# A scheduler's model of PSUM banks and the shared port, and a new early order, in a retention and feed-forward kernel

## The chip, the cores and the metric

One core of one Trainium2 chip. The metric is the device time of one execution in microseconds; a kernel's time is the median of its runs. TensorE (PE) multiplies matrices into PSUM, VectorE (DVE), ScalarE (ACT) and GpSimd (POOL) work element by element, and SyncE (SP) issues the DMAs.

## What is computed

The reference, cut to what matters (8 batches, 8 heads, 576 positions, head size 64; 4608 tokens of 512, inner width 2048):

```
scores = q @ k.T / sqrt(64)                       # per batch and head
ret    = scores * D        # D[i,j] = gamma_h**(i-j) for i >= j, else 0
x      = (ret @ v), heads side by side            # 4608 x 512
h      = x @ w_in                                 # 4608 x 2048
P      = a0 + a1*h + a2*h**2 + a3*h**3
Q      = 1 + |b0|*|h| + |b1|*h**2
out    = (P / (Q + 1e-6)) @ w_out                 # 4608 x 512
```

## The kernel before

**Tiling.** Tokens are taken in 36 units of 128; four units make a batch `b` of 512 tokens (nine batches). Retention is done unit by unit with a running state `S_sb` that fades from one unit to the next. The feed-forward part runs in steps `(b, f)`: one 512-token batch by one of 16 slices of 128 inner columns. Each step has a first product (`gemm1` and `gemm1_lo`, 12 matmuls of 128x512 into a PSUM bank `h`), a chain of elementwise instructions on ScalarE, VectorE and POOL, and a second product (`gemm2` and `gemm2_lo`, 12 matmuls into the accumulators `acc`). The order of the steps is: batch 0, slices 0 to 7; batch 1, all 16; batch 0, slices 8 to 15; then batches 2 to 8. Operands are split into a high and a low part (`xhi`, `xlo`, `w[0]`, `w[1]`, `g[0]`, `g[1]`), hence three times four matmuls.

**Weights** come as 64-bit words and are made into two parts on the chip: `begin` and `digit` (ScalarE), `join` (VectorE, `c<-bits`), `high_part` (ScalarE, `w<-c`), `low_part` (POOL, `w<-c,w`).

**The elementwise chain of an early step** (`feed_forward`, line 717; early means step number `i` below 24): `p_begin` (ScalarE, `p<-h`), `size` (ScalarE, `u<-h`), `p_mul` and `p_mul2` (VectorE, `p<-p,fac,h`), `v_line`, `v_mul`, `log`, `exp`, `quot`, `check`, `better`, then the high part `g_hi` (`g<-p`) and the low part `g_lo` (`g<-p,g`) of the result. Early steps keep the value of `v_line`, `log`, `exp` and `check` in the `h` bank itself, and so hold the bank until `better` is done. `V_POOL` names the early steps whose `v_mul` runs on POOL (then `v_line` writes to `v` and not to the bank). Steps with `i % 4 >= 2` among the early ones use two more banks of the pool `ps_w`. After step 23 those two banks are given to the late retention visits (unit 8 onwards, `late_visit`, line 640): the first visit has all the last instructions of such steps in its list of what it follows (`held`).

**The early units** 0 to 7 are done in `attention` (line 384): `scores`, `decay`, `outputs`, `cross` (with the state so far), then `keep_hi` (ScalarE, `xhi<-ps`), `keep_lo` and `grow` (VectorE, `xlo<-ps,xhi` and `S_sb<-S_sb,ps`), all on one PSUM tile, and `fade` on POOL.

**What sets the order.** No order is written by hand. Every piece of work is a `Task` with an engine (or a choice of two), a cost, a due time and the tasks that it follows. `Plan.run` (line 127) plays the five engines' queues forward with these costs: for each engine it works out the earliest start of each open task, takes among those within `SLACK` of the earliest the one with the smallest due time, and then the engine whose choice starts first; the task's instructions are emitted there and then, in this order. So a wrong estimate of a start changes the order in which the instructions stand in the queues; it never removes a wait that correctness needs. The due time of an early step's task is the step's number plus a constant of `DUE`; later steps use `STEADY`; the units use `FIRST`; weights `LEAD` and `AHEAD`; loads go in the order of `LOADS` (a number is the q/k half of a unit, a number with v its k/v half, w0 to w11 the first weight slices, gq the factors). `HOLD` says by how much longer a task must wait before the second engine of its choice may take it. `LAG` is what is added to a task's end before another may follow it.

**The port** (lines 58 and 157 to 159). Tasks marked `shared` use the SBUF port that VectorE and POOL have in common. Before, a VectorE task may start `PORT` = 0.33 us after POOL's shared task ends, a POOL task at once when VectorE's ends. **The banks:** before, nothing in the planner says that ScalarE and VectorE may not be on one PSUM bank together; `size` and `p_mul` both follow `p_begin` alone.

All instructions are issued through one helper, so nearly all rows of the profile show line 77; the names of the tiles tell them apart.

Of the kernel before, what the change touches and what calls it, by code (L numbers as in the profile page):

```python
# [33 lines left out]
EARLY = 8  # L34
DENSE = 8
VISITS = ()
V_POOL = (0, 1, 2, 3, 4, 5, 10, 11, 17)
IN_BANK = 24
WARM = 11
AHEAD = -5.306  # L40
REACH = 7.4
FIRST = (-62.53, -91.46, -10.84, -82.81, -41.01, -22.3, -1.16, -35.8)
UNITS = (20.48, 2.58, -2.5)
LATE = {'scale': -1.0, 'decay': 0.201, 'middle': 0.3, 'grow': 0.524, 'fade': 0.6, 'keep_hi': 0.3, 'keep_lo': 0.5}
LEAD = -2.163
CNV = 3
SHIFT = 60
LOADS = 'gq 0 mask 1 0v 2 1v 2v 3 w0 5 3v 5v w2 w1 w5 4 w4 6 w3 w6 4v w9 w7 w11 w10 7v 7 6v w8'.split()


def begin_of(name):
# [3 lines left out]
LAG = {'PE': 0.21, 'ACT': 0.138, 'DVE': 0.118, 'POOL': 0.08, 'SP': 0}  # L55
BACK = {'PE': 0.21, 'ACT': 0.0, 'DVE': 0.0, 'POOL': 0.0, 'SP': 0.0}
ENTER = {'PE': 0.03, 'ACT': 0.0, 'DVE': 0.0, 'POOL': 0.045, 'SP': 0.0}
PORT = 0.33
FETCH = ((4.8, 1.0), (15.5, 1.1))
DUE = {'p_begin': -0.998, 'size': 1.908, 'p_mul': -0.347, 'p_mul2': 5.296, 'v_line': 1.475, 'v_mul': 1.541, 'log': 3.284, 'exp': -0.985, 'quot': 1.963, 'check': 2.017, 'better': -1.338, 'g_hi': 1.445, 'g_lo': -1.676, 'gemm2': 4.596, 'begin': -0.512, 'digit': 1.055, 'join': -0.091, 'high_part': 1.387, 'low_part': 6.778, 'scale_q': 0.308, 'scale_v': 1.347, 'scores': 2.952, 'decay': 0.786, 'outputs': 6.305, 'cross': -5.06, 'keep_hi': -5.352, 'keep_lo': 3.008, 'grow': -0.794, 'fade': 1.051}  # L60
STEADY = {'p_begin': 0.5, 'size': 0.727, 'p_mul': 0.7, 'p_mul2': 0.93, 'v_line': 0.797, 'v_mul': 0.806, 'log': 1.578, 'exp': 1.838, 'quot': 1.6, 'check': 1.65, 'better': 0.79, 'g_hi': 1.888, 'g_lo': 2.167, 'gemm2': 3.44}
HOLD = {('POOL', 'scale_v'): 8.559, ('DVE', 'p_begin'): 0.394, ('DVE', 'high_part'): 0.99, ('DVE', 'g_hi'): 3.232, ('DVE', 'keep_hi'): 1.752, ('DVE', 'g_lo'): 106.303, ('DVE', 'low_part'): 1.696, ('POOL', 'v_mul'): 3.234, ('DVE', 'scale_q'): 1.067}
SLACK = {'PE': 0.19, 'ACT': 0.283, 'DVE': 0.2, 'POOL': 0.006, 'SP': 0.301}

ADJ = {}
# [3 lines left out]
class InOrder:  # L69


    def __init__(self, tc, engine):
        self.tc, self.engine = tc, engine
# [24 lines left out]
class Task:  # L98


    def __init__(self, due, ways, after, takes, gives):
        self.due, self.ways, self.takes, self.gives = due, ways, list(takes), list(gives)
        self.after = [t for t in after if t is not None]
        self.next, self.open, self.end, self.engine = [], 0, None, None


class Plan:
# [4 lines left out]
        self.tasks = []  # L112
        self.clock = dict.fromkeys(SLACK, 0.0)

    def add(self, engine, due, cost, emit, after=(), takes=(), gives=(), shared=False, other=()):
# [4 lines left out]
        t = Task(due + ADJ.get(len(self.tasks), 0), ways, after, takes, gives)  # L120
        self.tasks.append(t)
        for ring, key in gives:
            n, _ = self.rings[ring].left.get(key, (0, 0.0))
            self.rings[ring].left[key] = n + 1, 0.0
        return t

    def run(self):
        wait = {e: [] for e in SLACK}

        def opened(t):  # L130
            for e in t.ways:
                wait[e].append(t)

        for t in self.tasks:
            t.open = len(t.after)
            for a in t.after:
                a.next.append(t)
            if not t.open:
                opened(t)
        clock = self.clock  # L140
        port = {"DVE": 0.0, "POOL": 0.0}
        dma, landed, left, now, reach = 0.0, [0.75] * OUTSTANDING, len(self.tasks), -2.0, REACH
        while left:
            best = None
            for e, queue in wait.items():
                found = []
                for t in queue:
                    if e != "SP" and t.due > now + reach:
                        continue
                    names = [r for r, _ in t.takes]  # L150
                    ready = [self.rings[r].ready(names[:j].count(r)) for j, r in enumerate(names)]
                    if None in ready:
                        continue
                    _, _, shared, hold = t.ways[e]
                    s = max([0.0, *ready, *(a.end + (-BACK[e] if a.engine == e else ENTER[e]) for a in t.after)]) + hold
                    s = max(s, clock[e], landed[-OUTSTANDING] if e == "SP" else 0.0)
                    if shared:
                        held = port["POOL" if e == "DVE" else "DVE"]
                        s = held + PORT * (e == "DVE") if held > s else s
                    found.append((s, t.due, t))  # L160
                if not found:
                    continue
                until = min(s for s, _, _ in found) + SLACK[e]
                s, _, t = min((f for f in found if f[0] <= until), key=lambda f: f[1])
                if best is None or s < best[0]:
                    best = s, e, t
            if best is None:
                assert reach < 1e6, [(t.due, t.ways) for q in wait.values() for t in q]
                reach *= 2
                continue  # L170
            reach = REACH
            s, e, t = best
            if e == "PE":
                now = max(now, t.due)
            for w in t.ways:
                wait[w].remove(t)
            left -= 1
            cost, emit, shared, _ = t.ways[e]
            t.engine = e
            for ring, _ in t.takes:  # L180
                self.rings[ring].take()
            if e == "SP":
                clock["SP"] = s + 0.47
                fetch = sum(x for at, x in FETCH if dma < at <= max(dma, s + 1.5) + cost)
                dma = max(dma, s + 1.5) + cost + fetch
                t.end = dma + 0.8
                landed.append(t.end)
            else:
                clock[e] = s + cost
                t.end = s + cost + LAG[e]  # L190
                if shared:
                    port[e] = s + cost
            emit()
            for ring, key in t.gives:
                self.rings[ring].give(key, t.end)
            for n in t.next:
                n.open -= 1
                if not n.open:
                    opened(n)
# [3 lines left out]
def retention_ffn(ctx: ExitStack, tc: tile.TileContext, qk, kv, w_in, w_out, masks, factors, out):  # L203
# [25 lines left out]
    add = plan.add  # L229
# [154 lines left out]
    def attention(n, d, gap, got, consts, prev):  # L384
        u, b = n % 9, n // 4
        key = f"u{n}"
# [102 lines left out]
        def at_(x):  # L489
            return d + gap * x  # L490
# [15 lines left out]
        th = add("ACT", at_(DUE["keep_hi"]), 0.495, keep_hi, done, [("xp", b)] if n % 4 == 0 else [], gives,  # L506
                 other=[("DVE", 0.6, keep_hi_v, False)])
# [8 lines left out]
    late_s, bank = {}, {}  # L516
# [200 lines left out]
    def feed_forward(i, b, f, begins, ends):  # L717
        key = b, f
        due = DUE if i < IN_BANK else STEADY
# [149 lines left out]
        tp = add("ACT", i + due["p_begin"], 0.57 if early else 0.66, p_begin, [t1], [("p", key)], other=[("DVE", 0.62, p_begin_v, False)] if early else [])  # L869
        tu = add("ACT", i + due["size"], 0.48, size, [tp], [("u", key)], [] if early else free_h)  # L870
        td = add("DVE", i + due["p_mul"], 0.66 if early else 0.6, p_mul, [tp])
        td = add("DVE", i + due["p_mul2"], 0.66, p_mul2, [td], [], [] if early else free_h)
# [84 lines left out]
    prev = {}  # L957
# [90 lines left out]
```

## Time and profile before

| | |
|---|---|
| median of 3 runs | 903.93 us |
| the three runs | 902.79, 906.62, 903.93 us |
| the profiled execution | 907.24 us, span 905.2 us |
| TensorE's mean granted clock in it | 0.994 of full speed |
| busy: TensorE, VectorE, ScalarE, POOL | 98%, 86%, 70%, 19% of the span |

The profile is one execution. The span runs from its first to its last instruction; the execution's own time holds 2.0 us more around it. Times of rows are microseconds from the start of the span unless marked ns. PE is TensorE's matmuls, PEld its weight loads. "xN" counts instructions; what stands in brackets is the idle time of that engine just ahead and who ended it. A granted clock of 1.00 is 2.4 GHz, 0.50 is 1.2 GHz.

### The profile page before, as it was taken

To read this page: it belongs to the slowest core of one execution; us is meant where nothing else is said; L and a number is where in the kernel's file an instruction comes from. 1 tells how busy PE (TensorE), PEld (TensorE's weight loads), DVE (VectorE), ACT (ScalarE), POOL (GpSimd) and SP (SyncE) were. 2 spreads that over 40 slices of the span, in tenths; PEclk is the share of its full clock that TensorE was granted. 3 is DMA by queue.
4 is the path that set the end of the run, shared out by engine and by line. 5 is a ranking of instruction groups with operands and counts; after the bars stand their busy time and mean duration, and the time that the engine had idled before them with its cause. 6 is when DMAs were issued, how large, how long until landed. Compare 5 with 4: busy or idle time off the path is not lost.

```text
span 905.2 us, 17712 instructions
## 1 busy us (share of the span) xinstructions
PE 887.2 (98%) x7350; PEld 732.3 (81%) x7350; DVE 777.4 (86%) x1175; ACT 636.4 (70%) x1017; POOL 173.0 (19%) x150
## 2 busy tenths in 40 slices
PE   7999999899999999999999999999999999999998
PEld 7777788788878888888888888888888888888886
DVE  4788888878899989998899889888889889888885
ACT  1898998865666667666766677667766777667775
POOL 4766654412201110111100111011100001000000
PEclk9999999989999999999999999999999999999999
DMA  9991000014220112111211131111311021001001
GB/s 355 408 407 61 0 1 1 1 41 159 95 82 20 52 59 94 48 47 59 95 47 48 59 106 48 48 47 48 105 34 38 30 90 47 1 2 46 1 1 47
DMA packets 22208, 67.40 MB, mean 74 GB/s; under 512 B 2160, under 2 KB 4080, under 8 KB 22128
## 3 DMA queue, kind: packets, MB, share of 16 engines
q1 hardware_dynamic: 22128, 66.28, 20.3%
q8 instruction: 57, 0.93, 0.4%
q14 instruction: 23, 0.19, 0.1%
HBM read 56.83 MB, written 9.44 MB: 73 GB/s over the span
## 4 chain that ended last, share of the span: by engine, by line
PE 80%; DVE 9%; ACT 8%; issue 1%; DMA 1%; POOL 1%; SPq 0%; ACTq 0%; DVEq 0%; POOLq 0%
PE h L77 36%; PE acc L77 36%; PE ps L77 8%; DVE p L77 4%; ACT h L77 2%; ACT bits L77 2%; DVE c L77 1%; ACT u L77 1%; DVE v L77 1%; ACT p L77 1%; DVE h L77 1%; DMA qk<-in_qk 1%; ACT w L77 1%; ACT g L77 1%; ACT xhi L77 0%
## 5 line engine op out<-in xcount | busy, mean ns | idle before, releaser
L77 PE MATMUL acc<-w,g 128*128 128x512 f32 x1632 | 396.1, 391 | 1.7 <-ACT o L77 1.4
L77 PEld LDWEIGHTS acc<-w,g 128*128 128x128 f32 x1632 | 307.3, 189 | 67.3 <-ACT o L77 2.2
L77 PE MATMUL h<-xhi,w 128*128 128x512 f32 x1152 | 311.5, 393 | 2.0 <-DVE p L77 1.6
L77 PEld LDWEIGHTS h<-xhi,w 128*128 128x128 f32 x1152 | 213.5, 188 | 48.8 <-DVE p L77 2.8
L77 ACT ACTIVATE p<-h,fac 128x512 f32<-128x512 f32 x141 | 107.6, 763 | 103.7 <-PE h L77 102.7
L77 DVE SCALAR_TENSOR_TENSOR p<-p,fac,h 128x512 f32<-128x512 f32 x192 | 142.2, 744 | 20.4 <-ACT u L77 12.3
L77 PE MATMUL h<-xlo,w 128*128 128x512 f32 x576 | 154.3, 390 | 0.0
L77 PEld LDWEIGHTS h<-xlo,w 128*128 128x128 f32 x576 | 108.1, 188 | 23.1
L77 ACT ACTIVATE g<-p 128x512 fp32r<-128x512 f32 x136 | 85.3, 627 | 54.1 <-DVE p L77 52.0
L77 DVE TENSOR_TENSOR p<-p,h 128x512 f32<-128x512 f32 x120 | 82.2, 685 | 43.2 <-ACT u L77 40.7
L77 ACT ACTIVATE v<-u,absb 128x512 f32<-128x512 f32 x129 | 105.3, 816 | 3.9
L77 ACT ACTIVATE u<-v 128x512 f32<-128x512 f32 x120 | 75.7, 631 | 40.5 <-DVE v L77 40.5
L77 DVE SCALAR_TENSOR_TENSOR p<-p,fac,u 128x512 f32<-128x512 f32 x120 | 92.8, 773 | 9.2 <-ACT u L77 5.4
L77 ACT ACTIVATE u<-h 128x512 f32<-128x512 f32 x144 | 84.9, 590 | 7.9 <-DVE p L77 6.2
L77 DVE TENSOR_TENSOR v<-v,u 128x512 f32<-128x512 f32 x120 | 85.1, 709 | 5.9 <-ACT v L77 5.4
L77 DVE SCALAR_TENSOR_TENSOR v<-v,u 128x512 f32<-128x512 f32 x120 | 90.2, 752 | 0.0
L77 DVE SCALAR_TENSOR_TENSOR p<-v,p 128x512 f32<-128x512 f32 x120 | 84.3, 703 | 3.4
L77 DVE TENSOR_TENSOR g<-p,g 128x512 fp32r<-128x512 f32 x112 | 78.4, 700 | 3.1 <-ACT g L77 1.0
L77 ACT ACTIVATE u<-u 128x512 f32<-128x512 f32 x120 | 75.4, 628 | 2.5
L77 POOL TENSOR_TENSOR qk<-qk,fac 128x512 f32<-128x512 f32 x36 | 49.3, 1369 | 96.8 <-DMA qk<-in_qk 96.5
L77 POOL TENSOR_TENSOR S_sb<-S_sb,fac 128x256 f32<-128x256 f32 x18 | 14.7, 814 | 186.7 <-DVE S_sb L77 186.7
L77 PEld LDWEIGHTS ps<-qk 64*64 64x64 f32 (+1 forms) x1024 | 36.9, 142 | 15.5 <-issue 10.5
(55 smaller groups left out, 743.0 us busy)
## 6 DMA issues: line engine op xcount, KB each, us to landing
qk<-in_qk SPq DMA_DIRECT2D x36, 512.0 KB, 3.9
kv<-in_kv SPq DMA_DIRECT2D x36, 512.0 KB, 5.3
bits<-in_w_in SPq DMA_DIRECT2D x16, 512.0 KB, 10.5
bits<-in_w_out SPq DMA_DIRECT2D x16, 512.0 KB, 10.2
out<-o SPq DMA_DIRECT2D x14, 512.0 KB, 3.0
out<-o SPq DMA_DIRECT2D x8, 256.0 KB, 2.2
x<-in_kv SPq DMA_DIRECT2D x7, 256.0 KB, 4.6
fac<-in_factors SPq DMA_DIRECT2D x1, 301.0 KB, 2.9
```

The costliest lines, as they stand in the source:

```text
L77: return lambda *a, **k: self.tc.keep_in_program_order(method(*a, **k))
```

## The change

The planner gets two new rules and nearly all constants of the early part new values. A task may name a PSUM `bank`; a ScalarE task on a bank may not start before the end of the last VectorE task on it, and the reverse. Named are `keep_hi`, `keep_lo` and `grow` of the early units, and `p_begin`, `size`, `p_mul` and `p_mul2` of every step. `PORT` becomes one constant for each side: a VectorE task may start 0.10 us before the end of POOL's shared task, a POOL task 0.04 us before the end of VectorE's. `V_POOL` goes from nine to seven steps; the order of the loads, the due times of the early steps, of the units and of the weights, and the holds change. `STEADY`, `UNITS`, `LATE`, `SLACK` and the costs stay as they are. No instruction is added; which engine of a pair does a task, and in which place of its queue, is the planner's.

```diff
-V_POOL = (0, 1, 2, 3, 4, 5, 10, 11, 17)
+V_POOL = (1, 2, 3, 9, 11, 17, 22)
-AHEAD = -5.306
+AHEAD = -5.672
-FIRST = (-62.53, -91.46, -10.84, -82.81, -41.01, -22.3, -1.16, -35.8)
+FIRST = (-35.05, -136.62, -18.07, -94.24, -38.78, -4.26, -13.82, -16.04)
-LEAD = -2.163
+LEAD = -3.391
-LOADS = 'gq 0 mask 1 0v 2 1v 2v 3 w0 5 3v 5v w2 w1 w5 4 w4 6 w3 w6 4v w9 w7 w11 w10 7v 7 6v w8'.split()
+LOADS = '0 gq 1 mask 0v 1v 2 w0 2v 3 3v 5v w2 5 w1 w5 4 4v w6 6 w8 w4 w3 6v w7 w11 7v w9 w10 7'.split()
-PORT = 0.33
+PORT = {"DVE": -0.1, "POOL": -0.04}
-DUE = {'p_begin': -0.998, 'size': 1.908, 'p_mul': -0.347, 'p_mul2': 5.296, 'v_line': 1.475, 'v_mul': 1.541, 'log': 3.284, 'exp': -0.985, 'quot': 1.963, 'check': 2.017, 'better': -1.338, 'g_hi': 1.445, 'g_lo': -1.676, 'gemm2': 4.596,
+DUE = {'p_begin': -2.604, 'size': 2.699, 'p_mul': -0.527, 'p_mul2': 6.442, 'v_line': -1.066, 'v_mul': 2.072, 'log': 3.165, 'exp': -2.24, 'quot': 1.803, 'check': 2.07, 'better': -3.106, 'g_hi': 0.509, 'g_lo': -1.637, 'gemm2': 3.917,
...
-HOLD = {('POOL', 'scale_v'): 8.559, ('DVE', 'p_begin'): 0.394, ('DVE', 'high_part'): 0.99, ('DVE', 'g_hi'): 3.232, ('DVE', 'keep_hi'): 1.752, ('DVE', 'g_lo'): 106.303, ('DVE', 'low_part'): 1.696,
+HOLD = {('POOL', 'scale_v'): 8.866, ('DVE', 'p_begin'): 0.153, ('DVE', 'high_part'): 1.173, ('DVE', 'g_hi'): 0.201, ('DVE', 'keep_hi'): 1.352, ('DVE', 'g_lo'): 107.142, ('DVE', 'low_part'): 2.714,
...
+        used = {}
...
+                    if t.bank is not None:
+                        s = max(s, used.get(t.bank, {}).get("ACT" if e == "DVE" else "DVE", 0.0))
                     if shared:
-                        held = port["POOL" if e == "DVE" else "DVE"]
-                        s = held + PORT * (e == "DVE") if held > s else s
+                        s = max(s, port["POOL" if e == "DVE" else "DVE"] + PORT[e])
...
+            if t.bank is not None:
+                used.setdefault(t.bank, {})[e] = t.end
...
-        tl = add("DVE", at_(DUE["keep_lo"]), 0.6, keep_lo, [th], [], gives)
+        tl = add("DVE", at_(DUE["keep_lo"]), 0.6, keep_lo, [th], [], gives, bank=key)
-            tg = add("DVE", at_(DUE["grow"]), 0.33, grow, [to, *done, prev.get("tx")], [], gives)
+            tg = add("DVE", at_(DUE["grow"]), 0.33, grow, [to, *done, prev.get("tx")], [], gives, bank=key)
...
-        td = add("DVE", i + due["p_mul"], 0.66 if early else 0.6, p_mul, [tp])
+        td = add("DVE", i + due["p_mul"], 0.66 if early else 0.6, p_mul, [tp], bank=key)
```

`keep_hi`, `p_begin`, `size` and `p_mul2` get `bank=key` in the same way. In `DUE` and `HOLD` the entries of retention, weights and scaling, left out here, change too.

## Rows read from the trace of the kernel before

**Rows 1.** the page, section 1: busy time and share of the span, by engine
```profile
PE 887.2 (98%) x7350; PEld 732.3 (81%) x7350; DVE 777.4 (86%) x1175; ACT 636.4 (70%) x1017; POOL 173.0 (19%) x150
```

**Rows 2.** waits of TensorE, whole span: us in total, times, longest us
```profile
PE ps L77 <- DVE p L77: 2.7, 1, 2.7
PE ps L77 <- POOL qk L77: 2.4, 2, 1.7
PE ps L77 <- DVE kv L77: 1.8, 1, 1.8
PE ps L77 <- POOL S_sb L77: 1.7, 3, 0.9
PE h L77 <- DVE p L77: 1.6, 2, 0.8
PE acc L77 <- ACT o L77: 1.4, 2, 1.2
```

**Rows 3.** TensorE's timeline: start us, us, instructions [idle before <-releaser]
```profile
104.11 0.73 PE L77 MATMUL acc<-w,g 128*128 128x512 f32 x2 [1.19 <-ACT o L77]
...
177.33 1.15 PE L77 MATMUL ps<-qk 64*64 64x64 f32 x32
181.15 1.12 PE L77 MATMUL ps<-kv 64*64 64x64 f32 x16 [2.67 <-DVE p L77]
182.20 5.49 PE L77 MATMUL acc<-w,g 128*128 128x512 f32 x12
```

**Rows 4.** windows, TensorE: length, busy (instructions), granted clock, DMA share, GB/s
```profile
181.15:182.20 1.05, 1.05 (x17) 0.50 0.00 0
...
184.90:187.60 2.70, 2.70 (x7) 0.50 0.00 0
```

**Rows 5.** the chain that ended last, 195 to 215 us: start us, us, what
```profile
203.54 2.75 PE acc L77 x12
```

**Rows 6.** timeline of all engines, 164 to 192 us, at one bank of `h`
```profile
169.17 0.60 ACT L77 ACTIVATE u<-h 128x512 f32<-128x512 f32 x1 [0.68 <-DVE p L77]
...
169.80 0.75 DVE L77 SCALAR_TENSOR_TENSOR p<-p,fac,h 128x512 f32<-128x512 f32 x1 [0.67 <-ACT u L77]
```

**Rows 7.** waits of all engines, 28 to 180 us
```profile
DVE p L77 <- ACT u L77: 8.4, 12, 1.0
```

**Rows 8.** timeline of all engines, 164 to 192 us, at the shared port
```profile
176.47 1.28 POOL L77 TENSOR_TENSOR w<-c,w 128x512 fp32r<-128x512 f32 x1 [0.92 <-ACT w L77]
176.52 1.78 DVE L77 TENSOR_TENSOR v<-v,u 128x512 f32<-128x512 f32 x1
```

**Rows 9.** groups of VectorE by form, 28 to 180 us: busy us, mean ns
```profile
L77 DVE SCALAR_TENSOR_TENSOR p<-h,p 128x512 f32<-128x512 f32 x23 | 15.9, 692 | 0.8
...
L77 DVE COPY S_sb<-ps 128x256 f32<-128x256 f32 x1 | 0.4, 424 | 0.6 <-PE ps L77 0.6
```

**Rows 10.** timeline of all engines, 0 to 30 us, the first two units
```profile
6.79 1.16 PE L77 MATMUL ps<-qk 64*128 64x128 f32 x16 [0.66 <-POOL qk L77]
...
8.33 1.27 POOL L77 TENSOR_TENSOR qk<-qk,fac 128x512 f32<-128x512 f32 x1 [1.60 <-DMA qk<-in_qk]
...
9.65 1.72 PE L77 MATMUL ps<-qk 64*128 64x128 f32 x16 [1.70 <-POOL qk L77]
```

**Rows 11.** windows, TensorE, behind the first wait; columns as in rows 4
```profile
9.65:12.65 3.00, 3.00 (x30) 0.57 1.03 421
```

**Rows 12.** timeline of all engines, 0 to 30 us, SyncE's issue of the masks
```profile
1.65 0.42 SPq L77 DMA_DIRECT2D mask_sb<-in_masks  x1
```

**Rows 13.** timeline of all engines, 0 to 30 us, VectorE at the fourth unit
```profile
23.28 0.42 DVE L77 TENSOR_TENSOR S_sb<-S_sb,ps 128x256 f32<-128x256 f32 x1 [1.67 <-ACT xhi L77]
23.62 1.71 DVE L77 TENSOR_TENSOR kv<-kv,fac 128x512 f32<-128x512 f32 x2
```

**Rows 14.** windows, all engines: length, busy us of each (instructions)
```profile
40.00:180.00 140.00, 134.83 (x720) 109.46 (x718) 121.42 (x174) 126.09 (x221) 82.85 (x66) 1.00 0.23 92
```

**Rows 15.** VectorE's timeline at the first late visit
```profile
190.43 0.42 DVE L77 COPY S<-ps 128x256 f32<-128x256 f32 x1 [0.83 <-ACT xhi L77]
```

More of the change, by code (lines that the diff above doesn't have):

```diff
@@ L57 @@
 ENTER = {'PE': 0.03, 'ACT': 0.0, 'DVE': 0.0, 'POOL': 0.045, 'SP': 0.0}
-PORT = 0.33
+PORT = {"DVE": -0.1, "POOL": -0.04}
 FETCH = ((4.8, 1.0), (15.5, 1.1))
-DUE = {'p_begin': -0.998, 'size': 1.908, 'p_mul': -0.347, 'p_mul2': 5.296, 'v_line': 1.475, 'v_mul': 1.541, 'log': 3.284, 'exp': -0.985, 'quot': 1.963, 'check': 2.017, 'better': -1.338, 'g_hi': 1.445, 'g_lo': -1.676, 'gemm2': 4.596, 'begin': -0.512, 'digit': 1.055, 'join': -0.091, 'high_part': 1.387, 'low_part': 6.778, 'scale_q': 0.308, 'scale_v': 1.347, 'scores': 2.952, 'decay': 0.786, 'outputs': 6.305, 'cross': -5.06, 'keep_hi': -5.352, 'keep_lo': 3.008, 'grow': -0.794, 'fade': 1.051}
+DUE = {'p_begin': -2.604, 'size': 2.699, 'p_mul': -0.527, 'p_mul2': 6.442, 'v_line': -1.066, 'v_mul': 2.072, 'log': 3.165, 'exp': -2.24, 'quot': 1.803, 'check': 2.07, 'better': -3.106, 'g_hi': 0.509, 'g_lo': -1.637, 'gemm2': 3.917, 'begin': -0.029, 'digit': 0.759, 'join': 0.047, 'high_part': 1.78, 'low_part': 6.704, 'scale_q': 1.543, 'scale_v': 4.227, 'scores': 2.624, 'decay': -1.249, 'outputs': 4.655, 'cross': -2.337, 'keep_hi': -5.517, 'keep_lo': 3.965, 'grow': 0.705, 'fade': 1.485}
 STEADY = {'p_begin': 0.5, 'size': 0.727, 'p_mul': 0.7, 'p_mul2': 0.93, 'v_line': 0.797, 'v_mul': 0.806, 'log': 1.578, 'exp': 1.838, 'quot': 1.6, 'check': 1.65, 'better': 0.79, 'g_hi': 1.888, 'g_lo': 2.167, 'gemm2': 3.44}
-HOLD = {('POOL', 'scale_v'): 8.559, ('DVE', 'p_begin'): 0.394, ('DVE', 'high_part'): 0.99, ('DVE', 'g_hi'): 3.232, ('DVE', 'keep_hi'): 1.752, ('DVE', 'g_lo'): 106.303, ('DVE', 'low_part'): 1.696, ('POOL', 'v_mul'): 3.234, ('DVE', 'scale_q'): 1.067}
+HOLD = {('POOL', 'scale_v'): 8.866, ('DVE', 'p_begin'): 0.153, ('DVE', 'high_part'): 1.173, ('DVE', 'g_hi'): 0.201, ('DVE', 'keep_hi'): 1.352, ('DVE', 'g_lo'): 107.142, ('DVE', 'low_part'): 2.714, ('POOL', 'v_mul'): 2.563, ('DVE', 'scale_q'): 1.924}
 SLACK = {'PE': 0.19, 'ACT': 0.283, 'DVE': 0.2, 'POOL': 0.006, 'SP': 0.301}
@@ L98, with __init__ @@
 class Task:
-    def __init__(self, due, ways, after, takes, gives):
-        self.due, self.ways, self.takes, self.gives = due, ways, list(takes), list(gives)
+    def __init__(self, due, ways, after, takes, gives, bank):
+        self.due, self.ways, self.takes, self.gives, self.bank = due, ways, list(takes), list(gives), bank
         self.after = [t for t in after if t is not None]
@@ L113, in __init__, with add @@
         self.clock = dict.fromkeys(SLACK, 0.0)
-    def add(self, engine, due, cost, emit, after=(), takes=(), gives=(), shared=False, other=()):
+    def add(self, engine, due, cost, emit, after=(), takes=(), gives=(), shared=False, other=(), bank=None):
         ways = {engine: (cost, emit, shared, 0.0)}
@@ L119, in add @@
                 ways[e] = c, f, sh, HOLD[e, emit.__name__]
-        t = Task(due + ADJ.get(len(self.tasks), 0), ways, after, takes, gives)
+        t = Task(due + ADJ.get(len(self.tasks), 0), ways, after, takes, gives, bank)
         self.tasks.append(t)
@@ L506, in attention @@
         th = add("ACT", at_(DUE["keep_hi"]), 0.495, keep_hi, done, [("xp", b)] if n % 4 == 0 else [], gives,
-                 other=[("DVE", 0.6, keep_hi_v, False)])
-        tl = add("DVE", at_(DUE["keep_lo"]), 0.6, keep_lo, [th], [], gives)
+                 other=[("DVE", 0.6, keep_hi_v, False)], bank=key)
+        tl = add("DVE", at_(DUE["keep_lo"]), 0.6, keep_lo, [th], [], gives, bank=key)
         x_ready[b] += [th, tl]
         if u != 8:
-            tg = add("DVE", at_(DUE["grow"]), 0.33, grow, [to, *done, prev.get("tx")], [], gives)
+            tg = add("DVE", at_(DUE["grow"]), 0.33, grow, [to, *done, prev.get("tx")], [], gives, bank=key)
             prev["fade"] = add("POOL", at_(DUE["fade"]), 0.62, fade, [tg], shared=True)
@@ L868, in feed_forward @@
         free_h = [(hring, key)]
-        tp = add("ACT", i + due["p_begin"], 0.57 if early else 0.66, p_begin, [t1], [("p", key)], other=[("DVE", 0.62, p_begin_v, False)] if early else [])
-        tu = add("ACT", i + due["size"], 0.48, size, [tp], [("u", key)], [] if early else free_h)
-        td = add("DVE", i + due["p_mul"], 0.66 if early else 0.6, p_mul, [tp])
-        td = add("DVE", i + due["p_mul2"], 0.66, p_mul2, [td], [], [] if early else free_h)
+        tp = add("ACT", i + due["p_begin"], 0.57 if early else 0.66, p_begin, [t1], [("p", key)], other=[("DVE", 0.62, p_begin_v, False)] if early else [], bank=key)
+        tu = add("ACT", i + due["size"], 0.48, size, [tp], [("u", key)], [] if early else free_h, bank=key)
+        td = add("DVE", i + due["p_mul"], 0.66 if early else 0.6, p_mul, [tp], bank=key)
+        td = add("DVE", i + due["p_mul2"], 0.66, p_mul2, [td], [], [] if early else free_h, bank=key)
         tv = add("ACT", i + due["v_line"], 0.6 if in_bank else 0.71, v_line, [tu, td] if in_bank else [tu], [("v", key)])
```

## The prediction

> **What bounds the kernel now.** I read the page's head first, then what TensorE waited for over the whole span, then the stretch with the longest wait. TensorE is busy for 98% of the span [rows 1], so a new order can win only what TensorE waits for, and what it loses to a lower clock. Its waits after the first load are few [rows 2]: in the first 25 us 2.4 us for POOL's scaling of q and k, 1.8 us for VectorE's scaling of v and 1.7 us for the fading of the state; between 70 and 106 us 1.6 us for an `h` bank that VectorE had not left and 1.4 us for an accumulator that ScalarE had not copied out (most of it at 104 us, [rows 3]); and one wait of 2.7 us. Their sum is 11.6 us; the other rows of the view come to 2.0, and 1.1 of that lies ahead of the first load. So the large second part, from 190 us on, can only be made worse.
>
> The single long wait costs more than its length. At 177.33 us TensorE begins the first late visit (unit 8): its 32 score matmuls end at 178.48, and the next ones need the two `ps_w` banks, which step 23 still holds; it waits 2.67 us for a product `p` on VectorE, step 23's last instruction `better` [rows 3]. From then to 187.60 us the granted clock is 0.50, the lower of the two levels (1.2 GHz), in three stretches in a row, the first and last of them in [rows 4]; the twelve matmuls of one second-product step take 5.49 us there [rows 3], where 2.75 us is the rule [rows 5]. What stood ahead of the fall was an engine that had run 1.15 us in 3.82 us. From 178.48 to 187.61 us are 9.13 us, and the work in it needs 2.75 + 0.55 (the 16 small matmuls at half their 1.12 us) = 3.3 us at full clock. The place costs 5.8 us.
>
> Why was the visit put there? The planner places it where it believes step 23 done. Step 23 is late for two reasons the planner cannot see. **The banks:** `size` of a step on ScalarE waited 0.68 us for the VectorE product on the same `h` bank, and the second VectorE product then 0.67 us for `size` [rows 6]; to the planner `size` and `p_mul` both follow `p_begin` and may run side by side. Between 28 and 180 us VectorE sat idle 8.4 us in 12 places behind a ScalarE write of `u`, which is the `size` that reads the bank [rows 7]. **The port:** `v_mul` of step 24 started on VectorE at 176.52 and took 1.78 us, since POOL held the port from 176.47 to 177.75 [rows 8]; alone an instruction of this size takes 0.69 us [rows 9]. ScalarE, in order, stood behind it, and so did step 23's chain.
>
> **The change part by part.** No wait and no instruction is added: the semaphores between the two engines on a bank are there already [rows 6]. What changes is the planner's arithmetic, and by it the order of every queue.
>
> *Port.* The blocked `v_mul` ends at 178.30; less 0.69 us it began in effect at 177.61, 0.14 us before POOL's end. The old constant lets VectorE begin 0.33 us after it, the new one 0.10 us before: 0.43 us nearer at each blocked instruction. (POOL behind VectorE moves from 0 to 0.04 us before the end: nothing.) The Trainium skill speaks against it: SBUF — State Buffer, section "A bandwidth-pool intuition that's wrong (but worth ruling out)", puts the loser of the port at the holder's end plus about 115 ns. The row has 0.14 us before the end, so the measurement decides. By the page the new constant would be some 0.2 us too early at each blocked instruction; ten such in the early part, an estimate, would be 2 us of VectorE, and the sum would be 1 us higher if half of it reached TensorE.
>
> *The visit at 177 us.* With both effects known the planner should see step 23's end some 2.5 us later and put ahead of the visit what was ready: a whole step of a first or second product, 2.75 us [rows 5], enough to cover 2.67. Bounds: 0 to 5.8 us won; I take 5.0, since the rest of the pattern (new step's ScalarE reads ahead of step 23's logarithm) keeps its due times in the steady table.
>
> *The waits from 70 to 106 us* are of the same kind [rows 2], 3.0 us. Bounds 0 and 3.0; I take half, 1.5, as nothing says which side each falls.
>
> *The first 25 us.* The load list now issues the first q/k before the factors, unit 1's before the masks, and unit 1's v before unit 2's q. The POOL scaling that TensorE waited 1.70 us for is itself waiting for unit 1's load [rows 10]; taking 160 KB of masks from ahead of it gains 0.4 us at the 421 GB/s of the loads there [rows 11]. The masks, issued at 1.65 us [rows 12], then come 1.2 us later (512 KB); I cost that at nothing, since `decay` needs the first scores too, which end at 7.95 [rows 10]; were that cover gone, it would be those 1.2 us at most. The 1.8 us for v is a bank wait once more: the fourth unit's v is scaled at 23.62, behind `grow`, which stands at the head of VectorE's queue for 1.67 us until ScalarE's `keep_hi` has left the same bank [rows 13]. A planner that knows when `grow` can start may scale v in that gap; part of the gap is the wait for the unit's own matmuls, so I take half, 0.9. The half clock behind the first wait (0.57 of full over 3 us of work, [rows 11]) costs up to 1.3 us. Bounds 0 and 6.5 us (1.7 + 1.8 + 1.7 + 1.3); I take 0.4 + 0.9 = 1.3.
>
> *Work moved between engines.* The hold on a VectorE `g_hi` falls from 3.232 to 0.201 us, so the 24 early steps will send part of their high parts there from ScalarE. POOL loses two `v_mul` (9 to 7), VectorE gains them at the 0.75 us of its form with a bank and a factor [rows 6]. No row shows a 512-wide VectorE copy; the nearest are the 256-wide copy at 0.42 us and the 512-wide two-input form at 0.69 [rows 9], and I take the latter, the nearest in size, for both. All 24 moved would cost VectorE 16.6 + 1.5 = 18.1 us on paper. Between 40 and 180 us VectorE is busy 121.4 of 140 us, ScalarE 126.1 [rows 14]: its idle 18.6 us would just cover that, but part of it is waiting within chains. Bounds: 0 and 8.8 us on TensorE (18.1 less half of 18.6); I take 1.0. The later preparation of weights (`LEAD`) I cost at nothing: no TensorE wait is on a weight [rows 2]; were that cover gone, each late weight would cost one join and one copy.
>
> **The sum.** The profiled execution took 907.24 us (span 905.2 and 2.0 around it): 907.24 − 5.0 − 1.5 − 1.3 + 1.0 = 900.4 us. It stands 3.3 us above the median of 903.93. If that surplus is the half clock of this one execution, the new median is 900.4; if it is in every profiled one, 897.1. I take the middle: **898.8 us**, 0.6% faster. A measurement of this kernel can tell about 0.5%, 4.5 us, from no change.
>
> **The rivals.** *The waits only move.* ScalarE and VectorE work at 90% and 87% of the time before 180 us; steps come no faster than they allow, and what TensorE gains at 177 us it waits for at the next bank. For it: ScalarE's share [rows 14]. Against: from 190 us TensorE is fed without waits. It keeps what the loads give and the term for 70 to 106 us, 1.9 of 903.9: 902.0.
>
> *The plan stays blind.* Only four of a step's instructions name their bank; `v_line`, `log`, `exp` and `check`, which in early steps also work in the `h` bank, do not, nor do the late visits, where VectorE waits 0.83 us for ScalarE on `ps` at 190.43 [rows 15]. Then step 23 is still placed too early, the wait and the half clock stay, and only the start's 1.3 us are won: 902.6. The Trainium skill, PSUM — Partial Sum Buffer, section "PSUM bank collisions raise a hardware error", says that any two of the three engines must keep apart on a bank, reads included; the waits agree, and by it the marked four are too few.
>
> *VectorE becomes the bound* (slower). Place: steps 8 to 23, from 60 to 180 us. If over 11 of the 24 `g_hi` go to VectorE (half of 18.6 us idle, less 1.5, over 0.69), its chain to `better` runs late, `h` banks come free late, and TensorE waits at each step. At the upper bound the term is 8.8 instead of 1.0 and the 5.0 are not won, as the visit waits for the same chain: 898.8 + 7.8 + 5.0 = 911.6.
>
> **How the numbers follow.** Forecast 0.48, its own range 892 to 899.4 (lower end: 907.24 − 5.8 − 3.0 − 2.6 − 3.3 = 892.5, with twice the start's term). Waits move 0.20, plan stays blind 0.15, both within 0.5%. VectorE the bound 0.17, from 908.4 to 911.6. So faster 0.48, same 0.35, slower 0.17. The range of 8 in 10 takes in the first three cases and leaves the fourth out: 892 to 908.
>
> **What would show it.** Right: no TensorE wait over 1 us between 150 and 200 us, granted clock 1.00 there, the waits on `h` and `acc` before 106 us at most half, unit 1's scores at about 9.2 us, some `g` copies on VectorE, and `v_mul` blocked less often behind POOL. Wrong: a wait of over 2 us at the first late visit again with the clock at 0.50 behind it; VectorE over 95% busy between 60 and 180 us with TensorE waiting for it at many steps; or a new wait for a weight or a load before 60 us.

## The result, and the profile after

The changed kernel takes 893.83 us in the median of four runs (892.65 to 894.63), the kernel before 904.65 (902.79 to 906.62; the three runs above and one more): a ratio of 0.9879, 95% interval 0.9854 to 0.9904, 1.2% faster. The forecast was 898.8 us in a range from 892 to 908: right in its sign and range, with about half of the size. The profiled execution took 892.65 us, span 890.9, against 907.24 and 905.2 before: 14.3 us of span.

The head of the page after answers to [rows 1]:

```profile
PE 881.5 (99%) x7350; PEld 729.2 (82%) x7350; DVE 782.6 (88%) x1177; ACT 631.0 (71%) x1015; POOL 179.6 (20%) x150
```

TensorE's busy time fell by 5.7 us with the same number of matmuls, and what is not busy from 18.0 to 9.4 us. These two make the 14.3. The busy part is the clock: a matmul at 1.2 GHz counts as longer. The waits of TensorE over the whole span (us in total, times, longest us) answer to [rows 2]:

```profile
PE ps L77 <- POOL qk L77: 1.1, 2, 0.6
PE unread L77 <- DVE S_sb L77: 1.1, 1, 1.1
PE acc L77 <- ACT g L77: 1.0, 1, 1.0
PE ps L77 <- DVE s L77: 0.8, 2, 0.5
PE ps L77 <- DVE kv L77: 0.5, 2, 0.3
PE ps L77 <- DVE xlo L77: 0.2, 1, 0.2
PE h L77 <- DVE s L77: 0.2, 1, 0.2
```

The list sums to 4.9 us where it was 13.6 (`unread`, a matmul on zeros ahead of the first load, is the same 1.1 us in both). The 2.7 us for `p`, the 1.6 us for an `h` bank and the 1.4 us for ScalarE's copying of an accumulator are gone; one new wait of 1.0 us stands at 880.6 us, near the end of the span. At the first late visit, TensorE's timeline (answering to [rows 3]) shows no idle time at all:

```profile
168.81 1.98 PE L77 MATMUL acc<-w,g 128*128 128x512 f32 x8
170.71 1.15 PE L77 MATMUL ps<-qk 64*64 64x64 f32 x32
171.69 0.63 PE L77 MATMUL ps<-kv 64*64 64x64 f32 x16
172.25 1.19 PE L77 MATMUL acc<-w,g 128*128 128x512 f32 x4
```

The 32 score matmuls run from 170.71 us and the next 16, which took 1.12 us after a wait of 2.67, follow at once in 0.63. Counted in the traces, 312 matmuls of first products stand ahead of these scores in both kernels, but 272 of second products where there were 260: twelve more, one whole second product. The windows (length, busy of PE, PEld, DVE, ACT, POOL, granted clock, DMA share, GB/s) answer to [rows 4] and [rows 11]:

```profile
9.65:12.65 3.00, 2.62 (x54) 2.48 (x56) 2.44 (x5) 0.60 (x1) 0.99 (x1) 1.00 1.02 416
25.00:160.00 135.00, 135.00 (x775) 111.36 (x774) 124.02 (x179) 129.44 (x227) 90.39 (x71) 1.00 0.35 139
160.00:180.00 20.00, 20.00 (x248) 16.53 (x247) 16.73 (x28) 13.38 (x23) 6.47 (x6) 1.00 0.01 2
180.00:200.00 20.00, 20.00 (x270) 16.51 (x272) 17.45 (x29) 13.93 (x24) 4.73 (x4) 1.00 0.47 160
```

TensorE is busy without a break from 25 to 200 us and the clock is 1.00 in all four. What changed in the other engines' queues shows in their waits between 28 and 180 us, which answer to [rows 7]:

```profile
ACT g L77 <- DVE p L77: 4.3, 2, 2.9
...
DVE p L77 <- ACT p L77: 3.5, 7, 0.7
...
DVE p L77 <- ACT u L77: 1.2, 2, 0.7
...
ACT u L77 <- DVE p L77: 0.4, 1, 0.4
```

The row for `size` waiting, of before, that the last one answers to:

```profile
ACT u L77 <- DVE p L77: 4.1, 7, 1.7
```

VectorE's waiting for `size` fell from 8.4 to 1.2 us, and `size`'s own waiting for a VectorE product from 4.1 to 0.4. Not all of it is saved: VectorE's waiting for `p_begin` (`DVE p <- ACT p`) rose from 1.1 to 3.5 us, and ScalarE's for a product ahead of `g_hi` (`ACT g <- DVE p`) from 3.3 to 4.3.

### The profile page after: what moved, and what is told of

The parts are those of the page before. It is cut to its first block, busy times and chain, and to the rows that moved or that the text cites. A ratio compares the mean times of both kernels' runs of the same rounds, so it can differ in the third digit from the quotient of the medians.

```text
span 890.9 us, 17688 instructions
## 1 busy us (share of the span) xinstructions
PE 881.5 (99%) x7350; PEld 729.2 (82%) x7350; DVE 782.6 (88%) x1177; ACT 631.0 (71%) x1015; POOL 179.6 (20%) x150
## 4 chain that ended last, share of the span: by engine, by line
PE 94%; DMA 2%; DVE 2%; ACT 1%; SPq 0%; issue 0%; POOL 0%; ACTq 0%
PE h L77 44%; PE acc L77 42%; PE ps L77 8%; DMA kv<-in_kv 2%; DVE p L77 1%; DVE v L77 0%; SPq L77 0%; DVE s L77 0%; DVE kv L77 0%; ACT v L77 0%; ACT p L77 0%; DVE g L77 0%; ACT g L77 0%; POOL qk L77 0%; ACT u L77 0%
## 5 line engine op out<-in xcount | busy, mean ns | idle before, releaser
L77 DVE SCALAR_TENSOR_TENSOR p<-p,fac,u 128x512 f32<-128x512 f32 x120 | 95.1, 792 | 2.7 <-ACT u L77 2.6
L77 DVE SCALAR_TENSOR_TENSOR p<-v,p 128x512 f32<-128x512 f32 x120 | 90.4, 753 | 4.0
L77 DVE TENSOR_TENSOR v<-v,u 128x512 f32<-128x512 f32 x120 | 83.1, 693 | 9.8 <-ACT v L77 6.0
L77 DVE SCALAR_TENSOR_TENSOR v<-v,u 128x512 f32<-128x512 f32 x120 | 88.1, 734 | 0.0
L77 POOL TENSOR_TENSOR qk<-qk,fac 128x512 f32<-128x512 f32 x36 | 54.5, 1514 | 62.6 <-DMA qk<-in_qk 57.4
L77 POOL TENSOR_TENSOR S<-S,fac 128x256 f32<-128x256 f32 x12 | 10.5, 878 | 214.7 <-DVE S L77 214.7
## 6 DMA issues: line engine op xcount, KB each, us to landing
bits<-in_w_in SPq DMA_DIRECT2D x16, 512.0 KB, 10.7
```

What stands on the lines that cost most here:

```text
L77: return lambda *a, **k: self.tc.keep_in_program_order(method(*a, **k))
```

## The experiments

The planner allows the two rules and the constants to be put in one by one. All ratios are to the kernel before, run again beside each of three sets: the first eight runs on one chip, the last four on another. Its median there was 905.7 to 906.0 us. The changed kernel was not run again in them; its 893.83 us stand beside 904.65 for the kernel before, so distances from it come out about 1 us smaller by the ratios than by the medians.

### Rules and constants, four of eight corners

The constants are the new values of `V_POOL`, `AHEAD`, `FIRST`, `LEAD`, `LOADS`, `DUE` and `HOLD`.

**Both rules, old constants.** The edit, on the changed kernel:

```diff
-V_POOL, AHEAD, FIRST, LEAD, LOADS, DUE, HOLD of the changed kernel
+V_POOL, AHEAD, FIRST, LEAD, LOADS, DUE, HOLD of the kernel before
```

> The planner's two new rules (bank, port) with all constants of before. Theory (the rules make the plan fit the chip, and the bank rule carries most of it): about half of the gain, 897 to 901 us, the 2.67 us wait at the first late visit and the half clock behind it gone or under 1 us, other waits as before or moved. Rival A (the new constants alone make the gain, the rules only went along with them): 902 to 907 us, no different from before within 0.5%. Rival B (any change of the arithmetic shuffles an order that was searched for another arithmetic): slower than before, 907 to 915 us, with waits in places where before has none.

Measured: 898.61 us, ratio 0.9921 (0.9901 to 0.9940). The theory's range holds it. With the constants of before, made for the other arithmetic, the truer arithmetic gave 0.8% at once.

**New constants, old arithmetic.**

```diff
-                    if t.bank is not None:
-                        s = max(s, used.get(t.bank, {}).get("ACT" if e == "DVE" else "DVE", 0.0))
                     if shared:
-                        s = max(s, port["POOL" if e == "DVE" else "DVE"] + PORT[e])
+                        held = port["POOL" if e == "DVE" else "DVE"]
+                        s = held + 0.33 * (e == "DVE") if held > s else s
```

> The new constants (loads, due times, holds, V_POOL) with the planner's arithmetic of before: no bank rule, VectorE 0.33 us behind POOL. Theory: the plan no longer fits, TensorE waits again for VectorE and ScalarE, 899 to 907 us, and most of it between 30 and 180 us. Rival A (the constants alone): 892.5 to 896 us, the same as the changed kernel. Rival B (any shuffle hurts): slower than 905 us.

Measured: 904.71 us, ratio 0.9992 (0.9978 to 1.0005): nothing. Rival A has fallen; under the old arithmetic the new loads, due times and sharing are worth nothing. Its waits of TensorE, and the row at the longest:

```profile
PE acc L77 <- ACT g L77: 6.0, 2, 4.5
PE ps L77 <- POOL qk L77: 2.5, 2, 1.4
PE h L77 <- DVE p L77: 1.1, 1, 1.1
```

```profile
157.82 4.61 PE L77 MATMUL acc<-w,g 128*128 128x512 f32 x12 [4.50 <-ACT g L77]
```

The twelve matmuls behind that wait of 4.50 us take 4.61 us where 2.75 is the rule [rows 5]: the half clock again, behind another wait. The late visit itself does not wait in this run; the twelve further matmuls of a second product stand ahead of it here too, so they come with the constants and not with the rules.

**No bank rule; old port rule.** Each is the changed kernel with one piece of the diff above: without the bank rule the first two lines marked - are taken out, with the old port rule the third gives way to the two marked +.

> The changed kernel without the bank rule alone (the port rule and all new constants stay). Theory (banks carry most): 897 to 904 us, near the run with the constants alone; a TensorE wait of over 1 us that ends with a VectorE or ScalarE instruction on a bank. Rival (the port rule carries most): 893 to 896 us.

> The changed kernel with the port rule of before (VectorE 0.33 us behind POOL's end, POOL at once) and the bank rule and all new constants. Theory (banks carry most, the port is a detail of 0.43 us in some ten places): 894 to 897 us. Rival (the port rule carries most): 898 to 905 us.

Measured: without the bank rule 898.79 us, ratio 0.9926 (0.9908 to 0.9944); with the old port rule 899.52, ratio 0.9929 (0.9912 to 0.9945). The first is inside the theory's range; the second is in its rival's. "The port is a detail" was wrong here: with the new constants each rule is worth some 5 us. Both runs have waits at the visits back. TensorE's timeline from the scores of the first late visit, without the bank rule, then with the old port:

```profile
174.16 1.15 PE L77 MATMUL ps<-qk 64*64 64x64 f32 x32
176.41 0.68 PE L77 MATMUL ps<-kv 64*64 64x64 f32 x16 [1.10 <-DVE p L77]
...
179.60 1.19 PE L77 MATMUL h<-xhi,w 128*128 128x512 f32 x4 [1.38 <-DVE p L77]
```

```profile
176.68 1.15 PE L77 MATMUL ps<-qk 64*64 64x64 f32 x32 [0.18 <-DVE p L77]
178.87 0.68 PE L77 MATMUL ps<-kv 64*64 64x64 f32 x16 [1.05 <-DVE p L77]
...
181.39 1.19 PE L77 MATMUL h<-xhi,w 128*128 128x512 f32 x4 [0.71 <-DVE p L77]
```

These waits are the smaller part of the loss. The scores begin 3.5 and 6.0 us later than in the changed kernel (170.71), with the same matmuls ahead of them, out of 5.4 and 7.6 us that the two spans (896.3 and 898.5) are longer.

### One rule on the constants of before

The edit is that of "both rules, old constants", and one of the two rules taken out as well. With the bank rule alone:

```diff
-                        s = max(s, port["POOL" if e == "DVE" else "DVE"] + PORT[e])
+                        held = port["POOL" if e == "DVE" else "DVE"]
+                        s = held + 0.33 * (e == "DVE") if held > s else s
```

With the port rule alone:

```diff
-                    if t.bank is not None:
-                        s = max(s, used.get(t.bank, {}).get("ACT" if e == "DVE" else "DVE", 0.0))
```

> The kernel before with the bank rule only (old port rule, all constants of before). If the two rules each carry about half of what they gave together (898.6 us): 900 to 903 us, VectorE's and ScalarE's waits for each other on `h` between 28 and 170 us (7.7 and 4.1 us before) down to under 3 us in sum. If the bank rule carries it all: 898 to 899.5. If only both rules together are worth something: 903 to 908.

> The kernel before with the port rule only (no bank rule, all constants of before). If each carries about half: 900 to 903 us, the waits on `h` as before (over 8 us in sum). If the port rule carries it all: 898 to 899.5. If it needs the bank rule: 903 to 908.

Measured: the bank rule alone 898.51 us, ratio 0.9927 (0.9909 to 0.9945); the port rule alone 903.43, ratio 0.9974 (0.9964 to 0.9983). On the old constants the bank rule carries all that both rules give (898.61), and the port rule adds nothing to it. The waits between 28 and 180 us, first with the bank rule alone, then with the port rule alone:

```profile
DVE p L77 <- ACT u L77: 5.7, 6, 1.9
...
ACT u L77 <- DVE p L77: 0.3, 1, 0.3
```

```profile
ACT u L77 <- DVE p L77: 6.6, 13, 1.2
DVE p L77 <- ACT u L77: 6.0, 11, 0.7
```

12.5 us of such waits before (8.4 [rows 7] and 4.1 of ScalarE for a product), 12.6 with the port rule alone, 6.0 with the bank rule: not under the 3 that was expected, but halved, and the part that fell on ScalarE is all but gone. The sum of these waits does not order the runs by time: it is 10.8 us without the bank rule and 3.7 with the old port (on the new constants), at 898.8 and 899.5 us. TensorE's timeline with the bank rule alone, at the first late visit:

```profile
172.13 1.97 PE L77 MATMUL acc<-w,g 128*128 128x512 f32 x8
174.04 1.15 PE L77 MATMUL ps<-qk 64*64 64x64 f32 x32
175.02 0.63 PE L77 MATMUL ps<-kv 64*64 64x64 f32 x16
175.58 3.02 PE L77 MATMUL acc<-w,g 128*128 128x512 f32 x12
```

TensorE's order here is that of the kernel before ([rows 3]: scores, 16 small matmuls, then twelve of a second product): no product has been moved ahead of the visit. The wait is gone since `better` of step 23 came sooner: its VectorE row begins at 172.53 us,

```profile
172.53 0.69 DVE L77 SCALAR_TENSOR_TENSOR p<-h,p 128x512 f32<-128x512 f32 x1
```

1.8 us before TensorE needs the bank. Counted from the end of the k-th group of twelve `h` matmuls to the end of the k-th `p<-h,p` on VectorE, the chain of steps 10 to 23 takes 14.1 us in the mean before, 14.8 with the port rule alone, 11.5 with the bank rule alone and 10.7 in the changed kernel. Step 23 by itself takes 16.2, 16.9, 11.8 and 11.7.

### The place at 177 us by itself

In the kernel before, one task more goes into the list that the first late visit follows, the second product of step 22. In TensorE's list this puts 28 matmuls more ahead of the visit, 12 of a first product and 16 of second ones, where the forecast spoke of one product:

```diff
         acc_last[b] = products[b, f, 1] = t2
+        if i == 22:
+            held.append(t2)
```

> The kernel before with one more task in the list that the first late visit follows: the second product of step 22; no other rule or constant changes. It measures the place at 177 us by itself. Theory (the place costs 2.67 us of waiting and 3.1 us of half clock in the profile, and part of the half clock in the other executions): no TensorE wait over 1 us there, clock 1.00, 898.5 to 902 us, and the chain of step 23 as long as before (14 us from the end of its first product to `better`). Rival (the waits only move): 903 to 906 us, with the wait at a later bank or at an accumulator.

Measured: 903.61 us, ratio 0.9986 (0.9972 to 1.0000). For this move the rival is right; a move of one product alone was not tried. TensorE's timeline and the granted clock (windows as in [rows 4]):

```profile
182.03 1.15 PE L77 MATMUL ps<-qk 64*64 64x64 f32 x32
183.01 0.63 PE L77 MATMUL ps<-kv 64*64 64x64 f32 x16
186.85 2.08 PE L77 MATMUL h<-xhi,w 128*128 128x512 f32 x4 [3.20 <-DVE p L77]
```

```profile
186.00:192.80 6.80, 5.95 (x92) 0.50 0.01 2
```

The visit no longer waits; the next first product does, 3.20 us for another VectorE product on an `h` bank (`p<-p,fac,h`, done at 186.79), and the clock falls behind it for about as long as before (6.8 us here; before, 6.45 us, from 181.15 to 187.60). The chain of steps 10 to 23 is unchanged, 14.1 us.

### Is it the rule, or any shuffle?

```diff
-LAG = {'PE': 0.21, 'ACT': 0.138, 'DVE': 0.118, ...
+LAG = {'PE': 0.21, 'ACT': 0.143, 'DVE': 0.123, ...
```

> The changed kernel with two planner constants moved by 5 ns: the lag of ScalarE from 0.138 to 0.143 us and of VectorE from 0.118 to 0.123. Both rules and all new constants stay; the model is as true as before, but the order of the two queues before 190 us shuffles about as much as without a rule. It is the control for the runs without one rule (898.8 and 899.5 us). If those lost 5 us because the planner is blind to something, this run stays at 893 to 896 us. If any shuffle of an order that was searched for costs that much, it comes to 897 to 901 us.

Measured: 893.89 us, ratio 0.9875 (0.9859 to 0.9892), against 893.83 for the changed kernel. In the traces, with the numbers of buffers taken off and the longest common order of two lists taken out, 31% of ScalarE's first 400 instructions and 25% of VectorE's stand elsewhere than in the changed kernel; in the runs without one rule it is 28% to 31% and 21% to 29%. So this shuffle under a true arithmetic cost nothing, and the 5 us that the runs without a rule lost are best put down to the rules. It is one shuffle, not many.

### Parts of the constants, parts of the bank rule

In the changed kernel, the load list alone goes back:

```diff
-LOADS = '0 gq 1 mask 0v 1v 2 w0 2v 3 3v 5v ...
+LOADS = 'gq 0 mask 1 0v 2 1v 2v 3 w0 5 3v 5v ...
```

> The changed kernel with the load order of before. It measures what the new list gives in the first 60 us: the prediction took 1.3 us for the start, most of it from the loads and the order together. Theory: 894.5 to 897 us, TensorE's waits before 30 us 1 to 3 us longer than the 2.7 us of the changed kernel, none of it further on. Rival (the loads carry most of what the constants give, some 4.8 us): 897.5 to 900 us.

Measured: 896.95 us, ratio 0.9906 (0.9884 to 0.9928), 3.1 us more than the changed kernel (2.4 by the ratios, whose intervals overlap). TensorE's waits, over the whole span, are longer at the start:

```profile
PE ps L77 <- POOL qk L77: 3.1, 2, 1.7
PE ps L77 <- DVE kv L77: 1.3, 1, 1.3
...
PE ps L77 <- POOL S_sb L77: 0.9, 1, 0.9
```

These three rows come to 5.3 us; in the changed kernel the same kinds come to 1.6. The new due times go with the new list, so a part may be their misfit.

For the next two the edits take `bank=key` off the three tasks of the units, or off the four of the steps, in the run with the bank rule alone, such as:

```diff
-        tl = add("DVE", at_(DUE["keep_lo"]), 0.6, keep_lo, [th], [], gives, bank=key)
+        tl = add("DVE", at_(DUE["keep_lo"]), 0.6, keep_lo, [th], [], gives)
...
-        td = add("DVE", i + due["p_mul"], 0.66 if early else 0.6, p_mul, [tp], bank=key)
+        td = add("DVE", i + due["p_mul"], 0.66 if early else 0.6, p_mul, [tp])
```

The first pair stands for steps only, the second for units only.

> The kernel before (old constants, old port rule) with the bank rule on p_begin, size, p_mul and p_mul2 of the steps alone. Theory (the gain of the bank rule is the shorter chain of a step between 60 and 180 us): 897 to 901 us, as with the whole bank rule (898.5), the chain of steps 10 to 23 at 11 to 12 us from the end of the first product to `better`, against 14.1 before. Rival (the early units carry it): 903 to 907 us.

> The kernel before with the bank rule on keep_hi, keep_lo and grow of the early units alone. Theory: 902.5 to 907 us, not to be told from before, the chain of steps 10 to 23 at 13.5 to 15 us, the wait at the first late visit still over 1 us. Rival (the early units carry it): 898 to 901 us.

Measured: steps only 897.64 us, ratio 0.9911 (0.9893 to 0.9930); units only 908.42, ratio 1.0028 (1.0015 to 1.0041). The steps carry it, though their chain, 12.9 us, fell less than expected. With the rule on the units alone the kernel is slower than before, and than the 902.5 to 907 us expected. Its longest waits of TensorE and the rows at the first two of them:

```profile
PE ps L77 <- POOL kv L77: 3.0, 1, 3.0
PE acc L77 <- ACT o L77: 3.0, 1, 3.0
...
PE ps L77 <- DVE p L77: 1.1, 1, 1.1
```

```profile
53.66 1.09 PE L77 MATMUL ps<-s,kv 128*64 128x128 f32 x16 [3.00 <-POOL kv L77]
...
106.93 4.50 PE L77 MATMUL acc<-w,g 128*128 128x512 f32 x12 [2.97 <-ACT o L77]
```

Two waits of 3.0 us begin at 50.7 and 104.0 us, longer than any wait of the kernel before; behind the second, twelve matmuls take 4.50 us. Its chain of steps 10 to 23 is 12.6 us, shorter than before, probably since the elementwise queues catch up while TensorE stands (not tried): the mean chain does not order the runs by time, and that part of the expectation was wrong. The chain of step 23 alone does tell whether the first late visit waits. It is 8.5 to 13.3 us in the eight runs whose visit follows at once, and 14.5 to 16.9 in the others (14.5 with units only, 14.6 without the bank rule, 14.8 with the old port; the moved visit, with 16.2, hands its wait on).

In the changed kernel, `V_POOL` and four holds of VectorE tasks go back (`low_part` is the fourth):

```diff
-V_POOL = (1, 2, 3, 9, 11, 17, 22)
+V_POOL = (0, 1, 2, 3, 4, 5, 10, 11, 17)
-HOLD = {... ('DVE', 'p_begin'): 0.153, ('DVE', 'high_part'): 1.173, ('DVE', 'g_hi'): 0.201, ...
+HOLD = {... ('DVE', 'p_begin'): 0.394, ('DVE', 'high_part'): 0.99, ('DVE', 'g_hi'): 3.232, ...
```

> The changed kernel with the V_POOL of before (nine products on POOL) and the holds of before on VectorE's p_begin, high_part, low_part and g_hi. The prediction feared that the new sharing loads VectorE (a loss of up to 8.8 us, 1.0 taken). Theory (the profile of the changed kernel shows one high part on VectorE, so the sharing is a small term): 893 to 897 us. Rival (the sharing is what the constants give): 897.5 to 900 us. Were the fear right, this run would be faster than 893.

Measured: 893.18 us, ratio 0.9864 (0.9845 to 0.9883). The interval covers the changed kernel's: the new sharing is worth nothing, and costs nothing that can be told. No run beat the changed kernel by more than that.

### The table

Medians in us, by rules and constants:

| | no rule | port rule | bank rule | both |
|---|---|---|---|---|
| constants of before | 905.7 | 903.4 | 898.5 | 898.6 |
| new constants | 904.7 | 898.8 | 899.5 | 893.8 |

Differences of about 1 us are not read, as the corners come from different sets. The bank rule is worth 5 to 7 us beside anything (7.2 and 5.2 without the port rule, 4.8 and 5.0 with it). The constants and the port rule go together: the new constants give 4.6 and 4.8 us where the port rule is in, and nothing where it is not; the port rule gives 5.9 and 5.7 us on the new constants, and 2.3 or nothing on the old ones. Of what the constants give, 2.4 to 3.1 us hang on the load list. In the profiled executions the gains divide by place: with the bank rule alone the visit's scores begin 3.3 us sooner than before, as much as the waits of 70 to 106 us, and the visit is clean, but nearly nothing is won in the first 60 us.

## Why the prediction was right or wrong

**What bounds the kernel** was read rightly: TensorE's waits and the lower clock were all that could be won, and the 14.3 us of span are those two (8.6 and 5.7).

**The visit at 177 us: the term came in, its reason only in part.** The text priced the place at 5.8 us, took 5.0, and said that the planner, knowing both effects, would put "a whole step of a first or second product" ahead of the visit. The place is clean, and a whole second product more does stand ahead of the visit. But it came with the constants (it stands there under the old arithmetic too), it is not needed (with the bank rule alone the wait goes with TensorE's order as it was) and not enough (without the bank rule the visit waits 1.10 us behind the same matmuls). That the number came in so near is partly luck. The 2.67 us were where a delay of ScalarE's and VectorE's queues came to light, and the larger cure is the order in those two queues: step 23's chain fell from 16.2 to 11.7 us. On the constants of before the bank rule does this by itself (11.8), on the new ones it takes both rules (14.6 and 14.8 with one). In the changed kernel `better` of step 23 ends at 169.78 us and the bank is needed at 171.69; without the further product, some 2.7 us of work, it would still have come about 0.8 us late, an estimate from these rows. The text had both causes, banks and port, and their rows; it drew the gain from TensorE's queue alone. "The waits only move" is what happened to the larger move at TensorE by hand, not to the change.

**70 to 106 us:** 1.5 of 3.0 us taken; all 3.0 came. Halving for want of a sign was the mis-sized step. The text called these waits of the same kind as the visit's, and that is not shown: they are gone with the port rule alone too, where the visit still waits (1.33 and 1.98 us), and with the bank rule on the steps alone one of 0.8 us stays where the visit does not wait.

**The first 25 us** is the term most under-sized: 1.3 us, of at most 6.5. The visit's scores begin 6.6 us sooner (170.71 against 177.33 [rows 3]) with a second product more ahead of them, 2.75 us [rows 5]. TensorE had thus won 9.4 us by then; 3.0 are those of 70 to 106 us, and 6.4 were won before 60 us. Of these, TensorE's waits for POOL and VectorE at its `ps` tiles, without the visit's, fell from 6.3 to 2.6 us in the views of waits, 3.7 us, and the half clock of up to 1.3 us behind the first wait [rows 11] did not come in the profiled execution; the last 1.4 us are not itemised (0.2 us of the text's 1.7 for the state stand at 55 us, not in the first 25). Unit 1's scores came at 8.39 us, not 9.2: the text counted the 0.4 us of the masks and left out what the list does for the rest of the first loads. The load run puts the list at 2.4 to 3.1 us of the median.

**Work moved between engines:** 1.0 us of loss taken, none came. The groups of VectorE by form in the changed kernel's first 190 us (busy us, mean ns of one):

```profile
L77 DVE CAST w<-c 128x512 fp32r<-128x512 f32 x1 | 1.0, 1047 | 0.0
...
L77 DVE CAST g<-p 128x512 fp32r<-128x512 f32 x1 | 0.4, 417 | 0.0
```

One high part `g` went to VectorE, not eleven, and took 0.417 us: as little as the 256-wide copy of [rows 9], not the 0.69 that was taken. A short hold is a permission; presumably ScalarE was nearly always as early (not tried). The rival on the slower side needed eleven.

**The port** got no term of its own; it stood in the visit's 5.0 us beside the banks. With the new constants it is worth 5.7 us, and most of that before the visit. Its constant was read rightly, and `v_mul` was blocked less often, as forecast: four plain `v<-v,u` products on VectorE took 0.70 us in the mean, where two took 1.23 before. In the changed kernel a VectorE product behind POOL (the timeline of all engines; POOL's row holds two instructions, one right behind the other):

```profile
164.04 2.54 POOL L77 TENSOR_TENSOR w<-c,w 128x512 fp32r<-128x512 f32 x2
...
166.37 0.77 DVE L77 TENSOR_TENSOR v<-v,u 128x512 f32<-128x512 f32 x1
```

The product ends at 167.14; less the 0.69 us of an unblocked one [rows 9] it began in effect at 166.45, 0.13 us before POOL's end at 166.58, where [rows 8] had 0.14. The some 115 ns behind the holder's end that the Trainium skill states (SBUF — State Buffer, section "A bandwidth-pool intuition that's wrong (but worth ruling out)") are for a GpSimd-fed transfer blocked by a VectorE copy; for VectorE behind POOL these rows have 0.13 us before the end, and they decide.

**"The plan stays blind"** did not come. Marking the four instructions of a step is enough for the gain (897.64 us with them alone). That the late visits stay unmarked costs nothing that shows: no wait of TensorE from 25 to 880 us is over 0.2 us. Marking them was not tried.

**The surplus of the profiled execution.** The text took the middle between "half clock of this one execution" and "in every profiled one". The profiled execution of the changed kernel lies 1.2 us below its median of 893.83, so the surplus of before was no rule. The forecast's sum for the profile was 900.4 us against 892.65; the missing 7.8 us are 0.8 of the visit, 1.5 of 70 to 106 us, 5.1 of the start and 1.0 of the sharing, together 8.4, less the new wait of 1.0 near the end; 0.3 of the rest is the time around the span (2.0 us before, 1.7 after).

## What to carry to other kernels

When an order comes out of a model of the queues, look first for waits in the trace that the model cannot express (here two engines on one bank, 12.5 us of them on engines off the path) and put them into the model before changing its constants: here the new constants gave nothing under the old model, and the old constants under the truer one gave 0.8%. Try the parts in all combinations where that is cheap: the port rule looked worthless beside the bank rule until the constants were changed with it. A long wait of the bounding engine may be only where a late queue comes to light; move the waiting work by hand once, and if the wait reappears one step on, look in the other queues, at the chain of the very step that is waited for. To see where time was won, compare when the bounding engine reaches the same place in its list; here that showed 6.4 us at the start, where the waits alone showed 3.7.

## What was not expected of the hardware

A wait of 2.67 us (before), 3.20 (the visit moved), 4.50 (constants alone) or 2.97 (units only) on TensorE was each time followed by a stretch at or near 0.50 of the clock, while the waits of 1.10 and 1.38 us without the bank rule were not: the mean granted clock of that whole run was 1.000. The length of the wait alone does not decide. The other wait of the run with units only, 3.00 us up to 53.66 us, was followed by a clock of 1.00; and with the port rule alone 0.50 followed a wait of 1.98 us, which stood 1.15 us of work behind one of 1.33.

VectorE's 512-wide copy with rounding took 0.417 us, where the two-input forms of that size take 0.67 to 0.75. The `w<-c` copy took 1.05: it ran beside POOL's scaling of `kv` and ended 0.28 us behind it, so less 0.417 us it began in effect 0.14 us before POOL's end, as the blocked products do.
